# Hash attention with a SiLU MLP on one core: the first head's loads in two parts on two queues, its value sum later, and another order of the query blocks

## Chip, core and metric

One core of one Trainium2 chip. The metric is the device time of one execution in microseconds (us), as a median of several executions. With it each execution has a *span*: the time from the first to the last instruction. Engines: PE (TensorE, matmuls), ACT (ScalarE), DVE (VectorE), POOL (GpSimd), SP (SyncE, which here only issues loads and stores).

## The reference, cut to what matters

```python
# q, k, v: (4, 8, 768, 64) f32; proj: (64, 6); w_in: (512, 2048); w_out: (2048, 512)
q_bits = einsum('bhsd,dk->bhsk', q, proj) > 0          # 6 hash bits of each query
k_bits = einsum('bhsd,dk->bhsk', k, proj) > 0          # and of each key
mask   = bucket(q_bits)[..., :, None] == bucket(k_bits)[..., None, :]
scores = where(mask, q @ k.T / sqrt(64), -1e9)
attn   = softmax(scores)                               # 32 heads of 768 x 768
x      = (attn @ v) as (3072, 512)
h      = x @ w_in
out    = (h * sigmoid(h)) @ w_out                      # (3072, 512) f32
```

## The kernel before

For each head q and k are transposed on PE, multiplied with `proj`, and the signs of the result are appended to q and k as seven further rows ("bit rows"), so that one matmul gives scores that are hugely negative where the hashes differ. A head has 9 *windows* of 512 columns. In each one PE makes scores, ACT the exponential, and three windows later PE the weighted sum with values ("AV"). A matmul of a small constant `dmat` with the sum of all values (the "value sum") gives a query without a matching key the mean of the values. The MLP fills PE between. The whole attention and MLP is one stream on PE, 96% to 100% busy by stage from about 9 us on; the change concerns the first 9 us, in which the first head of 32 is prepared.

```python
    def load_first(h):                       # whole q and k of one head: 192 KB each, SP queue
        for n, src in (("q", q), ("k", k)):
            if h == 0:
                qk_sb[0, n] = ld.tile([P, 2, NJ * D], F32, tag=f"ld{n}", name=f"{n}_row")
            nc.sync.dma_start(out=qk_sb[0, n][:, h],
                              in_=src[0, h].rearrange("(p t) d -> p (t d)", p=P))
    # ... cut ...
    for i in range(2):
        load_first(i)
        load_v(0, slice(i, i + 1))
    load_qk(1)
    load_v(1)
    # ... cut ...
    def warm_up(n):                          # fills PE until data is there
        for _ in range(n):
            nc.tensor.matmul(wps, warm, warm[:, None, :].to_broadcast([P, 4, P]),
                             start=True, stop=True)
    warm_up(5)
    # ... cut: identity, constants, t_first (transposes), cast_first ...
    def proj_first(h):                       # hash projection and signs
        bp = ps.tile([P, 512], F32, tag="m", name="bp_ps", bufs=3)
        for c in range(4):
            e, n = divmod(c, 2)
            x0 = (2 * h + n) * HS
            o = e * (NBIT + 1)
            nc.tensor.matmul(bp[32 * c : 32 * c + 32, 0:HS], pw[:, o : o + 32],
                             qk32[0][:, x0 : x0 + HS], start=True, stop=True)
        bt = btp.tile([P, S], F16, tag="bits", name="bits")
        nc.vector.tensor_scalar(out=bt[:, 0:HS], in0=bp[:, 0:HS],
                                scalar1=sc[:, 0:1], scalar2=sc[:, 1:2],
                                op0=ALU.is_gt, op1=ALU.subtract)
        return bt
    # ... cut ...
    def v_unit(p, heads=(0, 1)):             # values to f16, and their sum, on POOL
        for i in heads:
            # ... cut ...
            nc.gpsimd.tensor_copy(out=vv[:, :, 0:D], in_=src)
            # three adds: vsa, vsb, vs
    # ... cut ...
    def parts(w):                            # which queries a window has
        h, r = divmod(w, NU)
        jp, j = divmod(r, 3)
        if j == 1:                           # queries 512-767 of two key blocks
            return h, [(2 * jp, 512, 256, 0), (2 * jp + 1, 512, 256, 256)]
        return h, [(2 * jp + j // 2, 0, 512, 0)]
    # ... cut: in av(w) ...
            if direct(h):                    # at window 0 of a head
                nc.tensor.matmul(o_ps[h][:, 0:NJ, :], dmat,
                                 vs[:, None, :].to_broadcast([P, NJ, E1]),
                                 start=True, stop=True)
    # ... cut: the order of work for the first head ...
    t_first(0, 0, nc.scalar.copy)
    t_first(0, 1, nc.vector.tensor_copy)
    warm_up(2)
    bt = proj_first(0)
    v_unit(0, (0,))
    # casts on ACT; bit rows on DVE, DVE, ACT, POOL
    t_first(1, 0, nc.scalar.copy)            # head 1, ahead of the first scores on PE
    t_first(1, 1, nc.vector.tensor_copy)
    warm_up(3)
```

The softmax here doesn't subtract the row's maximum and nothing guards it: scores larger than these inputs give would overflow.

## Time and profile before

| | before |
|---|---|
| time, median of 3 runs | 304.34 us (304.14 to 304.92) |
| profiled execution: time, span | 304.54 us, 302.8 us |
| head 0's k landed | 3.90 us |
| first exponential, first AV | 8.42 us, 9.07 us |

Read the profile from the whole to the part: the shares of the engines say which one bounds the kernel, busy times by stage say where that engine is not full, and the chain of work that ended last, in the first 10 us, says what each step there waited for. In a line of the chain the columns are start, length, and engine with tile and source line. The lines themselves stand in the prediction.

### The profile page before, as it was taken

What the parts mean: (1) busy time and instruction counts of PE and PEld (TensorE: products, weight loads), DVE (VectorE), ACT (ScalarE), POOL (GpSimd) and SP (SyncE); (2) the same over time, 40 slices, a digit from 0 to 9 for tenths busy, and PEclk for the clock granted to TensorE, in tenths of its full rate; (3) what the DMA queues carried; (4) which work ended last, traced back from release to release, by engine and by line L of the source; (5) the groups of instructions that cost most, each with busy time, mean ns of one, the idle gap of its engine ahead of it and who ended that gap; (6) DMA issues with size and microseconds to landing.
All of it is one profiled execution on the core that took longest, in us unless ns stands there. A gap on an engine that the chain in (4) does not pass through costs nothing.

```text
span 302.8 us, 7181 instructions
## 1 busy us (share of the span) xinstructions
PE 297.2 (98%) x2710; PEld 175.1 (58%) x2710; DVE 180.3 (60%) x344; ACT 210.2 (69%) x392; POOL 128.3 (42%) x203
## 2 busy tenths in 40 slices
PE   8999999999999999999999999999999999999996
PEld 3675855545665665555565665555566654446653
DVE  5797848899668454854695434854543442764332
ACT  5987989979887686878886766878877732452300
POOL 7589999286617561845149411765111100000000
PEclk9999999999999999999999999999999999999999
DMA  7999997979988737844068226011022003001112
GB/s 195 246 251 196 187 164 123 244 124 163 160 180 137 116 106 194 132 92 134 3 125 131 62 61 202 1 42 31 2 61 63 6 32 95 35 2 69 37 66 73
DMA packets 103170, 32.87 MB, mean 109 GB/s; under 512 B 90656, under 2 KB 100192, under 8 KB 103136
## 3 DMA queue, kind: packets, MB, share of 16 engines
q1 hardware_dynamic: 98752, 28.22, 44.1%
q0 software_dynamic: 4224, 4.19, 9.0%
q8 instruction: 21, 0.34, 0.5%
q14 instruction: 13, 0.11, 0.1%
q10 hardware_dynamic: 160, 0.00, 0.0%
HBM read 27.27 MB, written 6.29 MB: 111 GB/s over the span
## 4 chain that ended last, share of the span: by engine, by line
PE 91%; DVE 6%; ACT 1%; issue 1%; POOL 0%; DVEq 0%; ACTq 0%; POOLq 0%
PE o_ps L496 26%; PE h_ps L461 24%; PE s_ps L366 19%; PE o_ps L398 12%; PE bp_ps L281 3%; DVE g L470 2%; PE tp_ps L185 2%; PE warm_ps L125 1%; PE o_ps L482 1%; ACT u L369 1%; DVE qk L246 1%; PE tp_ps L198 1%; DVE qka L343 1%; PE bp_ps L225 1%; PE o_ps L389 0%
## 5 line engine op out<-in xcount | busy, mean ns | idle before, releaser
L369 ACT ACTIVATE u<-s_ps 128x512 f16<-128x512 f32 x288 | 157.1, 602 | 37.7 <-PE s_ps L366 37.2
L470 DVE SCALAR_TENSOR_TENSOR g<-th,h_ps 128x512 f16<-128x512 f32 x96 | 65.7, 689 | 75.0 <-ACT th L468 75.0
L461 PE MATMUL h_ps<-xT,win 128*128 128x512 f16 (+1 forms) x512 | 97.7, 325 | 0.8 <-DVE g L470 0.8
L398 PEld LDWEIGHTS <-u 128*128 128x128 f16 x1152 | 68.1, 98 | 41.8 <-ACT u L369 8.2
L496 PE MATMUL o_ps<-wout,g 128*128 128x512 f16 x368 | 91.6, 379 | 0.0
L468 ACT ACTIVATE th<-h_ps 128x512 f32<-128x512 f32 x96 | 58.0, 604 | 38.0 <-PE h_ps L461 35.5
L398 PE MATMUL o_ps<-vv,u 128*128 128x65 f16 x1152 | 82.6, 194 | 0.7 <-ACT u L369 0.4
L461 PEld LDWEIGHTS <-win 128*128 128x128 f16 x512 | 49.8, 98 | 32.3 <-issue 1.6
L418 POOL TENSOR_TENSOR x_pr<-osum,rec 128x384 f16<-128x384 f32 x23 | 19.0, 826 | 89.7 <-DVE rec L417 89.2
L496 PEld LDWEIGHTS <-g 128*128 128x128 f16 x368 | 35.8, 98 | 33.6
L366 PE MATMUL s_ps<-qka 71*128 71x512 f16 x192 | 52.6, 327 | 0.1
L366 PE MATMUL s_ps<-qkb 128*128 128x512 f16 x192 | 52.5, 326 | 0.0
L251 POOL TENSOR_SCALAR qka<-qk 64x1536 f16<-64x1536 f32 x15 | 22.0, 1466 | 11.5 <-DVE qk L246 6.5
L501 DVE TENSOR_SCALAR osb<-o_ps 128x512 f32<-128x512 f32 x23 | 15.8, 688 | 15.0 <-PE o_ps L496 15.0
L251 POOL TENSOR_SCALAR qkb<-qk 64x1536 f16<-64x1536 f32 x15 | 22.1, 1471 | 1.2
L262 POOL TENSOR_TENSOR vsa<-v_sb 128x192 f32<-128x192 f32 x32 | 18.9, 592 | 0.0
L260 POOL CAST vv<-v_sb 128x384 f16<-128x384 f32 x32 | 16.2, 507 | 1.8 <-DMA v_sb<-in_v_dram 1.4
L246 DVE STREAM_TRANSPOSE qk<-k_blk 128x768 f32<-128x768 f32 x10 | 15.9, 1589 | 0.3 <-issue 0.3
L246 DVE STREAM_TRANSPOSE qk<-q_blk 128x768 f32<-128x768 f32 x10 | 15.9, 1594 | 0.0
L366 PEld LDWEIGHTS <-qka 71*128 71x128 f16 x192 | 15.5, 97 | 0.7 <-ACT qka L238 0.6
L366 PEld LDWEIGHTS <-qkb 128*128 128x128 f16 x192 | 15.4, 97 | 0.0
L412 DVE TENSOR_TENSOR osum<-o_ps,vsum 128x390 f32<-128x390 f32 x23 | 13.0, 565 | 2.3
(70 smaller groups left out, 162.9 us busy)
## 6 DMA issues: line engine op xcount, KB each, us to landing
out_dram<-osb SPq DMA_DIRECT2D x23, 256.0 KB
v_sb<-in_v_dram SPq DMA_DIRECT2D x15, 384.0 KB
q_blk<-in_q_dram SPq DMA_DIRECT2D x40, 96.0 KB
k_blk<-in_k_dram SPq DMA_DIRECT2D x40, 96.0 KB
win<-in_moe_w_in_dram POOLq DMA_DIRECT2D x4, 512.0 KB, 8.0
wout<-in_moe_w_out_dram POOLq DMA_DIRECT2D x4, 512.0 KB, 6.3
q_sb<-in_q_dram SPq DMA_DIRECT2D x5, 384.0 KB
k_sb<-in_k_dram SPq DMA_DIRECT2D x5, 384.0 KB
```

The costliest lines, as they stand in the source:

```text
L246: nc.vector.transpose(out=dst, in_=qk_sb[p, "qk"[n]])
L251: nc.gpsimd.tensor_scalar(out=dst[rows, :], in0=qk32[p][rows, :], scalar1=CS, scalar2=1.0, op0=ALU.mult, op1=ALU.mult)
L260: nc.gpsimd.tensor_copy(out=vv[:, :, 0:D], in_=src)
L262: nc.gpsimd.tensor_tensor(out=sa, in0=src[:, 0:3], in1=src[:, 3:6], op=ALU.add)
L366: nc.tensor.matmul(sp[:, o0 : o0 + n], t[rows, S + jt * P : S + (jt + 1) * P], t[rows, c0 : c0 + n], start=True, stop=True)
L369: nc.scalar.activation(out=u, in_=sp, func=AF.Exp, scale=ESC)
L398: nc.tensor.matmul(o_ps[h][:, c0 // P + i, :], u[:, o0 + i * P : o0 + (i + 1) * P], vv[:, jt, :], start=(not direct(h) and w % NU == 0 and ...
L418: (nc.vector if direct(h) else nc.gpsimd).tensor_tensor(out=x_pr[p][:, :, par * D : (par + 1) * D], in0=o[:, 0:NJ, 0:D], in1=rec[:, :, Non ...
L461: nc.tensor.matmul(hp[:, j, :], w_in16[:, dt, ft * P : (ft + 1) * P], xT[4 * b + dt][:, c0 : c0 + n], start=(dt == 0), stop=(dt == NDT - 1))
L468: nc.scalar.activation(out=th, in_=hp, func=AF.Tanh, scale=0.5)
L470: after.append(lambda: nc.vector.scalar_tensor_tensor(out=g[ci][:, grp * f : (grp + 1) * f, :], in0=th, scalar=1.0, in1=hp, op0=ALU.add, o ...
L496: nc.tensor.matmul(o2[tt], g[ci][:, ft, ct * P : (ct + 1) * P], w_out16[:, ft, :], start=(ft == 0), stop=(ft == NFT - 1))
```

## The change

Its intent is to start the first head on two thirds of its data. The SP queue brings 256 of the 384 columns of head 0's q and k; the POOL queue brings the rest. Transposes, casts and the projection of the first part can then go ahead. To let the first two windows do without the rest, queries 512 to 767 come third in a group, not second. The value sum of head 0 is moved out of the way of the bit rows on POOL, and its matmul to window 4. The warm-up between the steps, after the first five pieces, is cut from 2560 columns to 640.

```diff
-    def load_first(h):
+    def load_first(h, cols=(slice(0, NJ * D),)):
...
+        for c in cols:
...
+                (nc.gpsimd if h == 0 and c.start else nc.sync).dma_start(
+                    out=qk_sb[0, n][:, h, c], ...)
...
+    load_first(0, (slice(0, 4 * D),))
+    load_v(0, slice(0, 1))
+    load_first(1)
...
     make_identity(nc, ident)
+    load_first(0, (slice(4 * D, NJ * D),))
...
-        if j == 1:
+        if j == 2:
             return h, [(2 * jp, 512, 256, 0), (2 * jp + 1, 512, 256, 256)]
...
-            if direct(h):
+        if direct(h) and w % NU == (0 if h else 4):
...
+    xa, xb = slice(0, 2), slice(2, 3)
+    t_first(0, 0, act, xa)
+    # casts of q's first part on ACT
+    warm_up(1)
+    t_first(0, 1, vec, xa)
+    # casts of k's first part on DVE
+    t_rest()                                  # one transpose each of q's and k's rest
+    # casts of the rest on ACT and POOL
+    v_unit(0, (0,), "v")                      # values to f16, without the sum
+    warm_up(3)
+    bpa, bpb = proj_first(0, xa), proj_first(0, xb)
+    signs_first(0, bpa, xa)
+    # bit rows of the first part on DVE, POOL, ACT
+    signs_first(0, bpb, xb)
+    # bit rows: ACT (first part), DVE, DVE, POOL, POOL (rest)
+    v_unit(0, (0,), "s")                      # the sum
+    t_first(1, 0, act)
+    t_first(1, 1, vec)
+    warm_up(1)
+    nc.vector.memset(QKB[1][0:64, :], 0.0)    # moved here
```

(Cut at the dots; comments stand for loops.)

## The prediction

> **What bounds the kernel now.** I read the page's shares first, then the busy time by stage, then the chain of work that ended last over the first 10 us, then the timelines and waits of single engines there, and last the DMA queues.
>
> The page's busy shares and its chain say that TensorE (PE) is the bound:
>
> ```profile
> PE 297.2 (98%) x2710; PEld 175.1 (58%) x2710; DVE 180.3 (60%) x344; ACT 210.2 (69%) x392; POOL 128.3 (42%) x203
> PE 91%; DVE 6%; ACT 1%; issue 1%; POOL 0%; DVEq 0%; ACTq 0%; POOLq 0%
> ```
>
> By stage, in busy us of each engine, the first 9 us are the part in which PE does little useful work (35 matmuls, of which 10 are warm-up); from 9 us on it is full:
>
> ```profile
> 0.00:9.00 9.00, 7.89 (x35) 3.33 (x35) 5.44 (x47) 5.31 (x10) 6.36 (x16) 1.00 0.76 200
> 9.00:16.00 7.00, 6.93 (x88) 4.51 (x89) 4.62 (x11) 6.28 (x13) 4.05 (x8) 1.00 1.27 246
> 16.00:27.00 11.00, 11.00 (x138) 7.83 (x135) 9.00 (x20) 9.33 (x18) 9.77 (x16) 1.00 1.20 244
> ```
>
> So a change in the first 9 us is worth what it moves the first weighted sum with values (line 398, at 9.07), and, PE being full from there to the end, a shift there should reach the end whole. The chain in the head (start, length, what):
>
> ```profile
> 1.01 2.31 PE warm_ps L125 x5
> 3.32 1.48 PE tp_ps L198 x6
> 4.80 0.79 PE warm_ps L125 x2
> 5.59 0.78 PE bp_ps L225 x8
> 6.37 0.90 PE tp_ps L198 x6
> 7.27 0.65 PE warm_ps L125 x3
> 7.92 0.09 issue
> 8.01 0.39 PE s_ps L366
> ...
> 8.42 0.61 ACT u L369
> ...
> 9.07 0.30 PE o_ps L398 x4
> ```
>
> The names hide that PE's warm-up there is filler: what is really waited for is data, then copies. The transposes of k waited for their load until 3.90, and everything after follows from it: the copy of k on VectorE (DVE) 4.84 to 5.40, hash projection 5.59 to 6.37, signs on DVE 6.44 to 7.12, bit rows to 7.9, first score 8.01, first exponential 8.42. From the waits and the timeline of ScalarE (ACT):
>
> ```profile
> PEld tp_ps L198 <- DMA k_row<-in_k_dram: 0.2, 1, 0.2
> ...
> 7.16 0.51 ACT L238 COPY qka<-bits 7x384 f16<-7x384 f16 x1 [0.25 <-DVE bits L228]
> 7.69 0.48 ACT L201 COPY qk<-tp_ps 128x384 f32<-128x384 f32 x1
> 8.42 2.06 ACT L369 ACTIVATE u<-s_ps 128x512 f16<-128x512 f32 x4 [0.25 <-PE s_ps L366]
> ```
>
> From k's landing (3.90) to the first exponential is 4.52 us. That interval is what the change shortens.
>
> **What the Trainium skill says.** "DMA: Bandwidth & Descriptors", section Latency and other measured facts, gives a first byte after about 0.6 us for a load from the SP queue and about 1 us for one from the POOL queue. The trace is slower on both: the first q load is issued at 0.74 and the queue has no packet before 1.6, and a POOL load of w_in issued at 28.95 (0.96 us of POOL) shows no packet until the slice 31.8 to 32.2; the second, issued at 36.67, shows its first ones between 38.5 and 39. So 1.9 to 2.9 us, for loads with more rows than the new ones. The same page, Issuing engines are not separate DMA queues, says that all queues interleave on the same 16 engines; the trace agrees in so far as both queues have packets in one slice (q0 is POOL's, share of 16 engines last):
>
> ```profile
> q0 software_dynamic: 20, 0.02, 89.6%
> q1 hardware_dynamic: 53, 0.06, 43.4%
> ```
>
> "TensorE: Matmul & The Clock Gate", Part 1, says the array starts at half clock and needs a busy window of about 3.4 us; Part 4 says transposes don't count as busy in the same way. The trace agrees with the first: six transposes take 1.48 us at 3.32 and 0.90 at 6.37, two warm-ups take 0.79 and three later 0.65. The projection, 0.78 at 5.59, takes 0.78 at 9.59 too, so full speed came between 4.8 and 5.6. No run here shows the second.
>
> **The change, part by part.**
> (1) Loads. The SP queue now brings 256 of 384 columns of head 0's q and k, 2 x 128 KB in place of 2 x 192. At the 237 to 258 GB/s of 2 to 4 us the 128 KB less are worth about 0.5 us: k's first part at 3.4. But PE is in warm-ups until 3.32 anyway. The rest, 2 x 64 KB, is issued from POOL after the identity, which ends at 1.46.
> (2) PE's order is: transposes of the first parts, then both transposes of the rest, a 384-column warm-up, and only then the projection of the first part. PE runs matmuls in order, so the projection waits for the POOL loads although it does not read them. This is the hinge. Their landing, an estimate: w_in's issue held POOL 0.8 to 1.0 us, so the second issue starts near 2.3; first packet 1.9 later, the lower end as there are fewer rows, 4.2; 64 KB at half of some 230 GB/s, 0.6. So L = 4.8.
> (3) From L: two transposes at half clock, 2 x 0.25, L+0.5; 384 columns of warm-up 0.2, L+0.7; projection of 256 columns, 0.78 x 2/3 = 0.52, L+1.2; signs: 0.68 less 128 columns at 1.0 ns (copies of 512 and 384 columns take 0.69 and 0.56), 0.55, L+1.85 with 0.1 to start. Then the bit rows: ACT has two in place of one, each about 0.39 (0.51 less 128 columns at 0.94 ns), L+2.65, then its copy of head 1, 0.48, L+3.15, then the exponential at L+3.2. PE meanwhile does the second projection (0.26), six transposes (0.90) and 128 warm-up columns: ready at L+2.45, so the first score is done by about L+2.9, before ACT is free.
> (4) Before, this interval is 4.52; now 3.2: 1.3 us less, from projecting two thirds, from casts done while the rest is still in flight, and from 512 + 3 x 512 columns of warm-up dropped. But it starts at 4.8 and not at 3.90: 0.9 us later. Net 0.4 us earlier: exponential at 8.0 in place of 8.42.
> (5) Value sum of head 0 late: POOL's three adds (0.60 + 0.32 + 0.32) come after the bit rows, and the matmul with the sum moves from window 0 to 4. It takes nothing from PE, as the matmul's 0.17 stays; it frees the way to the first bit row on POOL.
> (6) Queries 512-767 third in a group: lets the first two scores start without the rest. In all 288 windows the columns and weight loads stay: two 256-column scores take 0.22 in the chain, as one of 512 does. Worth 0 in the steady part, give or take 0.2 from where MoE units fall.
> Sum: 304.34 - 0.4 = 303.9.
>
> **Rivals.**
> A: the POOL loads land late and take the place of the wait removed. For it: 2.9 us to the first packet in one case, and the SP queue keeps the DMA engines 83 to 95% busy from 2 us on. Against: a quarter of the rows. At L = 5.6 the exponential starts at 8.8 and the time is 304.7.
> B: POOL becomes the bound of the head. Its two memsets (2.69 us at 1.40) now follow the issues, ending near 5.7; then two casts (0.3 each), the value cast (0.51) and the key bit row (0.37), at 7.3, just where PE is ready (L+2.45 = 7.25). Each 0.1 more on POOL above that is 0.1 later. At worst 304.4.
> C: the clock is released one window later, since 2560 columns of warm-up became 640 and PE may idle before the rest lands. It would add 0.5 to 0.8 us to projection and transposes and double the first scores: 305.2. Against: the five big warm-ups stay. Some 15%.
> D: the head gets faster but the gain is lost later, as ACT is 90% busy from 9 to 16 us. Against: it is also ahead, and PE has no slack to give back a shift to. The opposite, all waits go well (L = 4.3), gives 303.4.
>
> **Range and chances.** Centre 303.9; A and C pull up by about 1, D's opposite down by 0.6, and the three runs before spread over 0.8 us. So 303.0 to 305.0. Two per cent is 6 us, far more than the 9 us head can give or take by these terms: faster 0.01, same 0.98, slower 0.01.
>
> **What would show it.** The DMA wait in the head should be on the POOL loads, at 4.5 to 5.2, ahead of the transposes of the rest; the projection should start at about 5.5 and take 0.5 + 0.3; the first exponential at 7.8 to 8.3 and the first weighted sum at 8.4 to 8.9; from there to the end the same length as before within 0.3 us. Wrong if the first exponential moves by more than 0.8 us either way, if the transposes after 6 us still take 0.25 each (rival C), or if the shift of the head and the shift of the end differ by more than 0.4 us.

## The result and the profile after

The changed kernel took 305.06 us, median of 4 runs (304.91 to 305.89); the kernel before took 304.38 in 4 runs beside it. The ratio is 1.0026, 95% interval 1.0003 to 1.0048: within 2%, but above the predicted 303.0 to 305.0, and slower where 0.4 us faster was expected. (A ratio is the mean time of one kernel's fast runs over the mean of the other's in the same rounds, so not quite the ratio of the medians quoted.) By means, 305.23 is 0.77 us more than 304.46.

The profiled execution took 305.89 us with a span of 303.8, so it is the slowest of the four, and it shows more of the loss than a usual one. First its page, shares and the chain by engine:

```profile
PE 296.3 (98%) x2716; PEld 175.5 (58%) x2716; DVE 181.1 (60%) x348; ACT 210.2 (69%) x394; POOL 130.6 (43%) x209
PE 88%; DVE 6%; ACT 2%; DMA 1%; issue 1%; POOL 0%; DVEq 0%; ACTq 0%; POOLq 0%
```

PE still bounds the kernel and is busy 0.9 us *less* than before, as warm-up was cut. But "DMA 1%" is new in the chain. The first stage of the changed kernel (bounds and length, then busy us and instructions of PE, PEld, DVE, ACT, POOL, then clock, DMA share and GB/s):

```profile
0.00:9.00 9.00, 6.10 (x37) 2.90 (x38) 4.33 (x47) 4.41 (x10) 6.41 (x16) 1.00 0.81 199
```

PE is busy 6.10 us of these 9 where it was 7.89, and not because it finished early. The chain of the changed kernel in its head:

```profile
1.48 0.77 POOL q_row L81
...
2.25 4.02 DMA k_row<-in_k_dram
...
6.31 0.33 PE tp_ps L216
6.64 0.16 PE warm_ps L131
6.81 0.61 PE bp_ps L248 x8
...
7.45 0.56 DVE bits L256
...
8.03 0.40 ACT qka L265
...
8.87 0.48 ACT qk L210
9.35 0.58 ACT u L399
...
9.97 0.29 PE o_ps L429 x4
```

A single transfer, 64 KB of k from the POOL queue, holds the chain from 2.25 to 6.27. All that follows is the sequence that the prediction named: transposes, projection at 6.81 (before 5.59), signs, two bit rows on ACT, ACT's copy of head 1, the exponential. (The chain counts an instruction from the moment at which nothing else held it, so its start can lie up to 0.1 us after the timeline's, which has this exponential at 9.32.) The first AV stands at 9.97 where it was at 9.07. The waits of PE and the DMA issues of the changed kernel (KB, and us from issue to landing) name the same transfer:

```profile
PEld tp_ps L216 <- DMA k_row<-in_k_dram: 1.6, 1, 1.6
```

```profile
q_row<-in_q_dram POOLq DMA_DIRECT2D x1, 64.0 KB, 3.0
k_row<-in_k_dram POOLq DMA_DIRECT2D x1, 64.0 KB, 4.0
```

And k's first part, with a third less in it, landed no earlier. Its transposes waited for it until 4.22 us in this profile, where the whole load had been there at 3.90 (start, us, what was done, and in brackets the idle time before and what ended it; first before, then after the change):

```profile
3.90 0.50 PEld L198 LDWEIGHTS tp_ps<-ident,k_row 128*128 128x128 f32 x3 [0.16 <-DMA k_row<-in_k_dram]
```

```profile
4.22 0.29 PEld L206 LDWEIGHTS tp_ps<-ident,k_row 128*128 128x128 f32 x2 [0.74 <-DMA k_row<-in_k_dram]
```

Both loads were issued at 1.19. In later profiles of the changed kernel this wait ended between 3.8 and 4.0, so 64 KB less of k brought nothing. q's first part did come a little sooner: the first weight load of its transposes starts at 3.00 in place of 3.24. In the first 3 us the SP queue started 210 packets (about one per row of a load) with 0.30 MB before, and 208 with 0.19 MB after. It is tempting to read a pace of rows from this, but the two counts agree only at that moment: by 2.25 us they are 45 and 107.

The shift of the first AV is 0.90 us, that of the span 1.0, and that of the time in this pair 1.35: 0.35 us of the loss lie outside the span, where no line of the profile is. In all runs of the two kernels the time outside the span is 1.78 us for the one before and 2.13 for the changed one (means).

### The profile page after: what moved, and what is told of

Its sections match the earlier page's. It is cut to its first block, busy times and chain, and to the rows that moved or that the text cites. A ratio compares the mean times of both kernels' runs of the same rounds, so it can differ in the third digit from the quotient of the medians.

```text
span 303.8 us, 7208 instructions
## 1 busy us (share of the span) xinstructions
PE 296.3 (98%) x2716; PEld 175.5 (58%) x2716; DVE 181.1 (60%) x348; ACT 210.2 (69%) x394; POOL 130.6 (43%) x209
## 4 chain that ended last, share of the span: by engine, by line
PE 88%; DVE 6%; ACT 2%; DMA 1%; issue 1%; POOL 0%; DVEq 0%; ACTq 0%; POOLq 0%
PE o_ps L528 26%; PE h_ps L493 24%; PE s_ps L396 18%; PE o_ps L429 12%; PE bp_ps L311 3%; DVE g L502 2%; PE tp_ps L193 2%; DMA k_row<-in_k_dram 1%; PE o_ps L514 1%; ACT u L399 1%; DVE qk L273 1%; DVE qka L373 1%; PE o_ps L420 0%; PE bp_ps L248 0%; DVE qkb L370 0%
## 5 line engine op out<-in xcount | busy, mean ns | idle before, releaser
L429 PEld LDWEIGHTS <-u 128*128 128x128 f16 x1152 | 66.8, 98 | 45.6 <-ACT u L399 8.2
L273 DVE STREAM_TRANSPOSE qk<-q_blk 128x768 f32<-128x768 f32 x10 | 15.8, 1579 | 0.0
L273 DVE STREAM_TRANSPOSE qk<-k_blk 128x768 f32<-128x768 f32 x10 | 15.8, 1577 | 0.0
```

Source lines behind the costliest of these rows:

```text
L273: nc.vector.transpose(out=dst, in_=qk_sb[p, "qk"[n]])
L429: nc.tensor.matmul(o_ps[h][:, c0 // P + i, :], u[:, o0 + i * P : o0 + (i + 1) * P], vv[:, jt, :], start=((h == 0 or not direct(h)) and w % ...
```

## Experiments

In what follows "before" is always the kernel before, run on the same chip; its mean is 304.70 to 304.82 us (304.46 in the four runs beside the first result), its mean span 302.93 to 303.05. Its own spans range over 302.4 to 303.7 us. after_again, rest_by_sp, proj_ahead, order_only, quiet_sp, late_and_order, parts_only and warm_small ran on chip 15, whole_loads, warm_fill, pool_early and split_only on chip 0, the others on chip 1. The theories: the rest of head 0 lands late from POOL's queue, and PE's order makes the projection wait behind it (T1 in the expectations); the loss sits in the steady part, from the new order of query blocks (T2); loads here cost by row and issue, so that a split brings nothing earlier (T3); less warm-up makes TensorE's clock rise late (T4); SP's loads, in flight at once, delay the rest (T5), or POOL's queue is slow by itself (T6).

All runs in one table: mean time and span, time outside the span, instructions that the page counts on DVE, and the ratio to before with its 95% interval.

| run | time | span | outside | DVE count | ratio |
|---|---|---|---|---|---|
| after_again | 306.29 | 304.15 | 2.14 | 348 | 1.0048 (1.0029 to 1.0066) |
| rest_by_sp | 305.97 | 303.80 | 2.17 | 348 | 1.0040 (1.0022 to 1.0058) |
| proj_ahead | 305.56 | 303.52 | 2.05 | 351 | 1.0027 (1.0011 to 1.0042) |
| order_only | 304.83 | 303.03 | 1.80 | 344 | 1.0003 (0.9984 to 1.0021) |
| whole_loads | 304.67 | 302.52 | 2.15 | 348 | 0.9993 (0.9979 to 1.0008) |
| warm_fill | 305.15 | 302.98 | 2.17 | 348 | 1.0009 (0.9994 to 1.0024) |
| pool_early | 305.37 | 303.23 | 2.13 | 348 | 1.0016 (0.9999 to 1.0034) |
| split_only | 306.23 | 304.45 | 1.78 | 344 | 1.0037 (1.0018 to 1.0056) |
| late_and_order | 305.13 | 303.35 | 1.78 | 344 | 1.0013 (0.9992 to 1.0033) |
| parts_only | 305.97 | 303.82 | 2.15 | 348 | 1.0045 (1.0014 to 1.0075) |
| warm_small | 304.80 | 303.03 | 1.78 | 344 | 1.0002 (0.9987 to 1.0017) |
| after_third | 304.88 | 302.75 | 2.13 | 348 | 1.0004 (0.9992 to 1.0016) |
| pad_dve | 305.44 | 303.30 | 2.15 | 347 | 1.0022 (1.0003 to 1.0040) |
| pad_pool | 304.55 | 302.80 | 1.75 | 344 | 0.9992 (0.9972 to 1.0012) |
| best | 304.58 | 302.80 | 1.78 | 349 | 0.9993 (0.9980 to 1.0006) |
| best2 | 304.02 | 302.22 | 1.80 | 349 | 0.9978 (0.9966 to 0.9991) |
| after_pad | 304.83 | 303.03 | 1.79 | 349 | 1.0012 (0.9992 to 1.0032) |

All results were correct. One run of after_pad (309.90) was slow and is left out; one of parts_only (307.15, at a clock of 0.994) lifts its mean by 0.4; quiet_sp, a single deliberately slow run, is told below.

### after_again: the changed kernel once more

No edit.

> The changed kernel unaltered, five rounds beside the kernel before, and a second profile. My theory (T1): PE's in-order queue holds the first hash projection behind the transposes of the rest, and the POOL loads of the rest land late and unevenly (6.27 us in the first profile, against 4.8 predicted), so head and total are about 0.6 us longer, with a spread between runs of some 0.5 to 1 us: median 305.0, and the first exponential of the profiled run at landing + 3.0 to 3.2 us. Rival (T2): the loss sits in the steady part, from the new order within a group; then the first exponential could be as early as before and the total still longer.

Measured: 306.37 us median, slower still, all six spans between 303.6 and 304.6. Its chain shows a second thing that can go wrong:

```profile
2.25 3.57 DMA k_row<-in_k_dram
...
6.66 1.44 PE bp_ps L248 x16
8.10 1.47 PE tp_ps L206 x6
```

The rest of k landed at 5.82, earlier than in the first profile. But the 16 projection matmuls took 1.44 us (PE's timeline gives 1.51 for them here, and 0.86 in rest_by_sp below), and six transposes 1.47, as slow as the six at 3.32 in the kernel before (1.48). The clock rose only after 9.5 (the packed trace keeps the clock's changes, which `prof` does not print: full speed from 10.01 on), and the first exponential stood at 10.14. That is rival C of the prediction, seen in one profile. The column of the granted clock does not show it (it reads 1.00 from 5 to 9.5 us in this trace too); the durations of equal instructions do. What follows: the loss has more than one source, and its size varies from execution to execution.

### rest_by_sp: the rest by the SP queue, right after the first parts

```diff
-                (nc.gpsimd if h == 0 and c.start else nc.sync).dma_start(
+                nc.sync.dma_start(
-    load_first(0, (slice(0, 4 * D),))
+    load_first(0, (slice(0, 4 * D), slice(4 * D, NJ * D)))
```

> The only edit: the rest of head 0's q and k (2 x 64 KB) is issued from the SP queue directly after the first parts, ahead of v. T1 (the POOL queue is what is late): the rest lands at about 4.3 to 4.8, the first exponential at 7.4 to 7.9, total 303.3 to 303.9. Rival T3 (early loads run at a pace per row and not per byte, so that four loads of 128 short rows land as late as four of long ones): the rest lands near 5.2, first exponential 8.3, total about 304.3, no gain over before. T2 (steady part): the head is early but the total stays near 305.

Measured: 306.02 us, by means 0.31 below the changed kernel and 1.15 above before. PE's wait for the rest ended at 5.15, and now head 1's k, whose issue had moved two places back in the queue, landed at 7.79 (start, us, engine and line, then in brackets the idle time before and what ended it):

```profile
7.92 0.52 PE L205 MATMUL tp_ps<-ident,k_row 128*128 128x128 f32 x3 [0.84 <-DMA k_row<-in_k_dram]
```

PE takes matmuls in order, and head 1's transposes stand ahead of the first scores; so these wait for a load that they don't read. The first exponential stood at 8.76. The expected 303.3 to 303.9 was missed: T1 alone doesn't hold. Without POOL's queue the rest is 0.7 us earlier than in after_again (same chip) and 1.1 earlier than in the first profile, but two more issues on SP's make a later load late.

### split_only: the kernel before, its first loads split in two by SP

```diff
-            nc.sync.dma_start(out=qk_sb[0, n][:, h], in_=... whole)
+        for c in (slice(0, 4 * D), slice(4 * D, NJ * D)) if h == 0 else ():
+            for n, src in (("q", q), ("k", k)):
+                nc.sync.dma_start(out=qk_sb[0, n][:, h, c], in_=...[:, c])
```

> The kernel before with one edit: head 0's q and k loaded in two parts each, all four by the SP queue; the work is as before and needs both parts. T3 (early loads run at a pace per row, issue by issue): the last part lands at about 5.1 in place of 3.9 to 4.0, head 1's k at 7.8 in place of 6.7; first exponential 9.2 to 9.6, total 305.3 to 305.7. If bytes set the pace: lands at 4.0 to 4.3, total under 304.8. Also looked at: the time outside the span (total less span), which is 1.8 us for before and 2.1 for the change: it stays at 1.8 if it has to do with the work in parts, and goes to 2.1 if with the number of loads.

Measured: 306.07 us, span 1.4 us above before. The work is that of the kernel before, and so are the bytes:

```profile
2.31 2.97 DMA k_row<-in_k_dram
...
6.65 1.44 PE bp_ps L230 x8
8.09 1.47 PE tp_ps L203 x6
```

k's last part lands at 5.28 in place of 3.90. PE idles for it, the clock rises late again (projection 1.44 where it took 0.78), and the first exponential stands at 10.92. That is later than the 9.2 to 9.6 expected, and the total exceeds 305.7, because of the clock. The landing is what T3 said, and the issue times say which half of T3 it is: whole, k was issued at 1.19 and landed 2.7 us later; its last part was issued at 2.31, as the fourth load, and landed 3.0 us later. So of the 1.4 us 1.1 come from the later issue, and a load of 64 KB takes no less time than one of 192. That is a pace of issues; a pace of rows is not shown apart from it. That k's first part is no earlier was seen in the changed kernel.

### quiet_sp: the rest from POOL while the SP queue is held

SP's other loads were made to wait for three tiny POOL memsets (into the tiles they fill), placed after POOL's two large ones, so that they start only after 5.5 us. Slow on purpose (310.97 us, one run): only the landing counts.

```diff
+    for t in (v_sb[0], qk_sb[0, "q"][:, 1:2], qk_sb[0, "k"][:, 1:2]):
+        nc.gpsimd.memset(t[:, :, 0:1], 0.0)
+    load_v(0, slice(0, 1)); load_first(1); ...    # moved here
```

> The changed kernel, with the SP queue's later loads (v, head 1, pair 1) held back behind three tiny memsets at the end of POOL's, so that POOL's two loads of the rest have the DMA engines nearly to themselves until about 5.5 us. One look, for the landing alone; the total will be several us worse on purpose. If traffic of the SP queue makes the landing late (T5): k's rest lands by 4.4 to 4.8 (2.2 to 2.5 us after its issue). If it is the software path itself (T6): at 5.5 to 6.3 as in the changed kernel, 3.3 us or more after the issue.

The DMA issue of this run:

```profile
k_row<-in_k_dram POOLq DMA_DIRECT2D x1, 64.0 KB, 2.5
```

Alone, the transfer takes 2.5 us from issue to landing, the length that the prediction had assumed (2.3 to 4.8). Beside SP's loads it took 4.0, 3.6, 2.8 and 2.8 us in four profiles of the changed kernel and of after_pad, whose loads are the same, and 3.6 in proj_ahead and 2.7 in warm_fill, which also share them. On chip 15, that of this run, the two profiles with SP's loads have 3.6, so T5 fits there with 1.1 us, from one profile; on chips 0 and 1 SP's loads add only 0.2 to 0.3, and T5's own forecast for after_third was missed (below). So SP's traffic is a part of the delay, and not shown to be all of it. In the first profile, of the 64 packets of POOL's queue three lie between 5 and 6 us, all others earlier, so that it was the last few that came late:

```profile
q0 software_dynamic: 3, 0.00, 1.7%
```

By the packed trace two of these three carry 4 bytes; in after_again the last four, at 5.1 to 5.5, all do.

### proj_ahead: the projection of the first part ahead of the rest

In the changed kernel, PE gets the projection of part one (and DVE, POOL, ACT its signs and bit rows) ahead of the transposes of the rest; the rest's copy and q casts go to DVE.

```diff
+    bpa = proj_first(0, xa)
+    signs_first(0, bpa, xa)
+    for n, e, copy in ((0, 0, vec), (1, 0, pool), (0, 1, act), (1, 1, act)):
+        bits_first(0, n, e, copy, xa)
     t_rest()
-    bpa, bpb = proj_first(0, xa), proj_first(0, xb)
+    t_first(1, 0, act)
+    bpb = proj_first(0, xb)
```

> POOL loads kept; the projection, signs and bit rows of the first part stand ahead of the transposes of the rest in the program, the copy and q casts of the rest go to DVE so that ACT's bit rows don't wait behind them. T1: the projection of the first part starts at 5.4 although the rest lands near 6; the first exponential at about 7.9 to 8.2 and hardly moves with the landing; total 303.7 to 304.1 and a smaller spread. If instead the landing is not what holds the head (T2, or POOL as the bound, rival B of the prediction), the first exponential stays near 9 and the total near 305.

Measured: 305.45 us; the expected 303.7 to 304.1 was missed. The projection ran at 4.92 to 5.56, as wanted, but DVE's two casts of k stood ahead of the signs and ended only at 6.17; the first exponential came at 8.72, not at 7.9 to 8.2, and the third score waited on DVE's bit rows until 8.96. The hinge that the prediction named was real, and opening it moved the wait to DVE.

### pool_early: POOL's issues ahead of its identity

```diff
+    load_first(0, (slice(4 * D, NJ * D),))     # right after the warm-up's memset
     warm_up(20)
     make_identity(nc, ident)
-    load_first(0, (slice(4 * D, NJ * D),))
```

> The changed kernel with the two POOL issues moved ahead of the identity, 0.5 us earlier. If the landing is a fixed time after the issue[...]: it comes 0.5 us earlier, at 5.3 to 5.8, and the total is 0.4 us below the change's. If it is set by the SP queue's traffic on the same DMA engines: it stays at 5.8 to 6.3, total unchanged.

Measured: 305.14 us. The issues came only 0.19 us earlier (1.30 in place of 1.49), not 0.5. PE's wait for k's rest ended at 4.92, below both forecasts; but without the edit the rest landed at 4.94 in warm_fill, so this run doesn't decide between them. The profiled execution had its first exponential at 8.20, a span of 302.6. What then held the chain was DVE:

```profile
5.08 1.28 DVE L235 TENSOR_SCALAR qka<-qk 64x256 f16<-64x256 f32 x2
```

Two casts take 1.28 us here, beside POOL's memset that runs to 5.83. In the first profile of the changed kernel they took 0.59, almost clear of that memset (5.40 to 5.99, memset to 5.51), and in after_third, half beside it, 0.94. "SBUF — State Buffer", section Who interferes with whom, says that DVE in its faster modes and POOL lock each other out of a shared port pair; the three durations agree with that, though no run shows in which mode these casts ran.

### warm_fill: more warm-up ahead of the rest

```diff
+    warm_up(12)
     t_rest()
```

> The changed kernel with 12 x 128 columns of warm-up put ahead of the transposes of the rest, where PE waits for POOL's loads anyway. Clock theory (T4: part of the loss, on this chip, is that the clock is released at about 10 us in more executions since warm-up was cut from 5120 to 3200 columns and PE idles): the slow executions (spans of 304.5) vanish, spans are 303.0 to 303.9, median total 305.3 to 305.7. If the clock has no part: as the change itself, 306.2, both levels still there.

Measured: 305.15 us, five spans of 302.7 to 303.5, mean as before. With PE kept busy, the clock was up before the projections of its profile (first 8 in 0.61 us). But the warm-up itself took until 5.90, after the rest had landed, and the first exponential stood at 9.02.

### warm_small: the kernel before with the changed kernel's small warm-ups

```diff
-    warm_up(5)
+    warm_up(20)     # pieces of up to four blocks of 128 columns, in all three places
-    warm_up(2)
+    warm_up(4)
-    warm_up(3)
+    warm_up(1)
```

(The memset of `QKB[1]` is moved too, as in the change.)

> The kernel before with only the change's small moves: warm-up of 4 x 128 and 128 columns in place of 2 x 512 and 3 x 512, and the second memset of a key tile moved from 3 us to after head 1's transposes. T4 (less warm-up lets the clock be released a window later in some executions): two levels of span, the upper near 304, mean span 0.2 to 0.6 above before's. If warm-up has no part: spans as before, 302.4 to 303.7. Outside the span 1.8.

Measured: 304.80 us, ratio 1.0002. Less warm-up by itself costs nothing, so T4 falls in its simple form.

The clock's changes in the packed traces say more. In the profiles whose head has before's loads and matmuls, full speed begins at 4.10 us (order_only), 5.40 (before), 6.00 (pad_pool), 6.79 (pad_dve) and 6.81 (late_and_order), and their spans follow it: 302.4, 302.8, 303.1, 303.4 and 303.5 us; so do the first exponentials, 8.20 to 9.10. So most of the spread of before, and half a microsecond either way in any single profile of a head, goes with the moment of the clock. Of the other profiles, quiet_sp apart, only after_again (10.01) and split_only (10.36) are later than 7.00. The records' stretches are whole multiples of 3.41 us. One such step before their rise, at 6.60 and 6.95, these two could have had it as late_and_order did; but PE, idle for a split load, had been busy for only 2.31 and 2.74 of the 3.41 us before, where it was busy for 2.85 or more before the first rise of every other profile that records one. So the late rise goes with two things together, where the steps of 3.41 us fall and how idle PE was. No experiment tests it, and one record doesn't fit so simply: quiet_sp stays at half speed until 17.68, although PE was busy all through the step from 10.85 to 14.27.

### order_only: the kernel before with queries 512 to 767 third

```diff
-        if j == 1:
+        if j == 2:
```

> The kernel before with one edit: queries 512-767 third in a group in all heads, nothing else. T1: worth nothing: 304.3 to 304.5, ratio to before within 0.0007 of 1, first exponential at 8.4 as before. T2 (the loss is in the steady part): 304.9 to 305.1, as the whole change.

Measured: ratio 1.0003, span as before; the first exponential of its profile stood at 8.20, with an early clock (above). No gain or loss of the order of the query blocks by itself is seen, as predicted, within the interval's 0.2%.

### late_and_order: that order and the late value sum, in the kernel before

```diff
+        if direct(h) and w % NU == (0 if h else 4):      # matmul with the sum, at window 4
-    v_unit(0, (0,))
+    v_unit(0, (0,), "v")
     # bit rows
+    v_unit(0, (0,), "s")
```

> The kernel before with the new order within a group and the late value sum of head 0, without loads or work in parts. By the prediction both are worth 0 on PE: mean span within 0.4 us of before. Also for the 0.35 us outside the span: 1.8 us outside if these have no part in it, 2.1 if they are its cause.

Measured: 305.29 us, ratio 1.0013 with an interval that holds 1. Its profiled execution had a late clock for this head (8 projections 1.38 us), so this says only that no gain of the late sum is seen in the kernel before.

### whole_loads: the changed kernel with whole first loads

```diff
-    load_first(0, (slice(0, 4 * D),))
+    load_first(0)
-    load_first(0, (slice(4 * D, NJ * D),))
```

> The changed kernel with one edit: head 0's q and k are loaded whole, each by one load of the SP queue, as before; the work in parts, the order and the late value sum stay. T1 (what costs is the landing of the split rest, and the interval of about 3.05 us from its landing to the first exponential is sound): the rest is there with the first parts at about 4.0, its transposes end by 4.9, the first exponential comes at 7.4 to 7.8, against 8.4 (8.2) before, and the span is 301.8 to 302.3 at an early clock release: total 303.8 to 304.2, at most that of before. Rival (working in parts is itself slower: more and smaller instructions on ACT, POOL and DVE): the first exponential stays at 8.5 or later, total over 305.

Measured: 304.83 us; the span fell to 302.52, 0.52 us below before (303.04), so everything in the change except the split is good for about half a microsecond of span, and the split is what costs. (The changed kernel did not run in this call. Beside before in its own calls its mean span was 1.10 longer in after_again and 0.27 shorter in after_third, which puts the split at 0.2 to 1.6 us.) The time gained only 0.15 by means, as 2.15 us lie outside the span. I had expected the exponential at 7.4 to 7.8. In the profiled execution (span 302.8) it was at 8.42, since a warm-up of 384 columns stood in PE's order between the landed data and a projection at half speed (the clock rose at 7.00):

```profile
5.22 0.32 PE warm_ps L131
5.54 1.06 PE bp_ps L247 x8
```

### parts_only: whole loads, work in parts, value sum early

```diff
-        if direct(h) and w % NU == (0 if h else 4):
+            if direct(h):                                # at window 0, as before
-    v_unit(0, (0,), "v")
+    v_unit(0, (0,))
-    v_unit(0, (0,), "s")
```

> The run with whole loads, but with the value sum back to early (before POOL's bit rows, and its matmul first in window 0). If the late sum matters as the prediction says (it frees POOL's bit row): POOL reaches its first bit row about 1.2 us later, the first exponential comes at 8.6 to 9.3 in place of 8.4, span about 0.4 to 0.8 longer than with whole loads and a late sum (302.5). Outside the span: 2.1 if the work in parts is the cause of the 0.35 us, 1.8 if the late sum is.

Measured: 305.62 us, span 1.3 us above whole_loads by means (0.9 without the run of 307.15), though not on the same chip. The chain shows POOL in the way:

```profile
7.91 0.32 POOL vs L294
...
8.29 0.40 POOL qka L264
...
8.74 0.40 PE s_ps L395
```

The bit row on POOL comes after the sum, and the score after the bit row. So the late sum is needed where the work goes in parts; where it doesn't, no gain was seen.

### after_third, pad_dve and pad_pool: the time outside the span

after_third is the changed kernel once more. The two others are the kernel before with tiny memsets that nothing reads:

```diff
+    pad = cst.tile([P, 4], F32, name="pad")
+    for i in range(3):                         # pad_pool: range(2), nc.gpsimd
+        nc.vector.memset(pad[:, i : i + 1], 0.0)
```

> The changed kernel again, a third profile, beside the best version on one chip. Traffic theory (T5): k's rest lands 3.5 to 4.1 us after its issue at 2.25, that is at 5.8 to 6.3; first exponential 9.0 to 9.4, or 10.1 where the clock comes late; mean span 303.1 to 304.2, 2.13 us outside it.

> The kernel before with three more tiny DVE memsets early, where DVE has slack. For the time outside the span alone: the work in parts has three DVE instructions more. If the number of DVE instructions makes the 0.35 us: 2.1 us outside; if not: 1.8. Span as before.

> The kernel before with two more tiny POOL memsets after the identity. For the time outside the span alone: the work in parts has two POOL instructions more. If their number makes the 0.35 us: 2.1 us outside; if not: 1.8. Span as before.

Measured: after_third 304.85 us beside 304.84 for before, though its span, 302.75, is 0.27 us *below* before's 303.02. In its chain the rest landed at 5.08, and the exponential stood at 8.16, close to the 8.0 predicted. Every forecast of T5 for this run (landing at 5.8 to 6.3, exponential from 9.0 on, span over 303.1) was missed on the early side:

```profile
2.25 2.83 DMA k_row<-in_k_dram
...
8.16 0.58 ACT u L399
```

pad_dve put the time outside the span from 1.78 to 2.15 us; pad_pool left it at 1.75. (By its page the changed kernel has four DVE and six POOL instructions more, not three and two, so pad_pool doesn't try its whole number.) Three memsets of one column at the start of the kernel are not work after its last instruction. So the changed kernel pays 0.35 us for its number of DVE instructions, or for how they are laid out, and not for what they do. The span of pad_dve (two runs) is within before's range.

### after_pad: the changed kernel with one more DVE instruction

```diff
+    pad = cst.tile([P, 4], F32, name="pad")
+    nc.vector.memset(pad[:, 0:1], 0.0)
```

> The changed kernel with one more instruction: a memset of 128 x 1 elements on VectorE that nothing reads, ahead of the loads. Its page will count 349 instructions on VectorE, as in best, instead of 348. If the 0.35 us that the changed kernel takes outside the span hang on how many instructions VectorE has (344 and 349 gave 1.78 us; 347 and 348 gave 2.15; 351 gave 2.05), the time outside the span falls from 2.13 to 1.78 us and the total from about 305.0 to about 304.6 us, with the span unchanged at 302.7 to 304.0 us. If they hang on something else in the changed kernel (the two issues from GpSimd's queue, more semaphores), the time outside stays at 2.13 us.

Measured: in its three fast runs the time outside the span is 1.79 us, as expected if the count matters. One instruction *more* takes 0.34 us *away*. By the count on DVE in all runs: 344 and 349 give 1.75 to 1.80 us, 347 and 348 give 2.13 to 2.17, 351 gives 2.05. The three fast runs gave 304.83 us on average, with a span of 303.03: no better in total than after_third, as the span happened to be 0.28 us longer.

### best and best2: keeping what helped

best is whole_loads without the warm-up ahead of the projection, and with one bit row on DVE instead of ACT. best2 also moves the value-sum matmul of *both* first heads to window 8 and, on POOL, puts head 1's casts ahead of the two sums.

```diff
     # best, against whole_loads
-    warm_up(3)
     bpa, bpb = proj_first(0, xa), proj_first(0, xb)
+    bits_first(0, 1, 1, vec, xa)               # was on ACT
     # best2, against best
-        if direct(h) and w % NU == (0 if h else 4):
+        if direct(h) and w % NU == (0 if h > 1 else 8):
-    v_unit(0, (0,), "s")
...
-        v_unit(0, (1,))
+        v_unit(0, (1,), "v")
+        v_unit(0, (0,), "s")
+        v_unit(0, (1,), "s")
```

> The run with whole loads, with two edits from its timeline: the 384-column warm-up ahead of the first projection goes, and the second key bit row goes from ACT to DVE (0.40 to about 0.22 us), so that ACT's copy of head 1 and the first exponential come 0.4 to 0.5 earlier. If the chain in the head sets the time: first exponential at 7.6 to 8.1 (8.42 with whole loads), mean span 301.9 to 302.3 (302.52), total 304.0 to 304.4, below before's mean of 304.8 by 0.1 to 0.3%. If another wait takes their place (POOL's bit row, bits of the second part): span as with whole loads.

> The kernel best (whole first loads; no warm-up between the transposes and the projection; the second key bit row on VectorE) with the value-sum matmul of both first heads moved to window 8, and on GpSimd head 1's key casts and value-bits work ahead of the two value sums. Best had its first exp at 7.86 us where the kernel before had 8.42, and had lost that lead by 15.8 us; the wait in its trace was PE's for GpSimd's value sum at 14.02 to 14.36 us, and a score that waited for VectorE's bits. If that wait is what gave the lead back, moving the matmul later keeps some of it: mean span 302.3 to 302.6 us where best had 302.80, time outside the span 1.78 us as in best, total 304.1 to 304.4 us, 0.4 to 0.7 below the kernel before. If the lead goes in another place (the order of ScalarE's and VectorE's work for the second pair of heads), the span stays at 302.7 to 302.9 us and the total at 304.5 to 304.7 us.

Measured: best 304.50 us with a span of 302.80, both short of what was expected, and an interval that holds 1. best2 304.01, better than expected, with all five runs between 303.91 and 304.16, below all nine of before (304.28 to 305.27). Best had its first exponential at 7.86, 0.56 ahead of before, and had lost it by 15.8. PE's timeline of best shows where, and below it that of best2:

```profile
14.36 0.33 PE L419 MATMUL o_ps<-vs,dmat 128*128 128x390 f16 x1 [0.17 <-POOL vs L294]
...
15.74 0.30 PE L428 MATMUL o_ps<-vv,u 128*128 128x65 f16 x4
```

```profile
13.46 0.33 PE L419 MATMUL o_ps<-vs,dmat 128*128 128x390 f16 x1
...
15.19 0.30 PE L428 MATMUL o_ps<-vv,u 128*128 128x65 f16 x4
```

In best, PE waited for POOL's sum of head 1. (Another 0.17 us of the lead went to head 0's sum matmul: in before it ran at 8.65, while PE waited for the first exponential; in best it stands in the full stream, at 11.29.) In best2 that sum is not waited for, and the AV that follows the hash projection of the second pair of heads starts at 15.19 and not at 15.74 (15.74 in the kernel before, too). The lead of 0.55 us reaches the end: mean span 302.22 against 302.93. Best2 beats before by 0.22% (interval 0.09% to 0.34%), and its slowest run lies below every run of the changed kernel, after_pad's among them.

## Why the prediction was wrong

**The bound, and that a shift of the head carries to the end: right.** First AV 0.90 us later, span 1.0 later. PE has no slack to give or take in the steady part, except where a new wait appears in the stage right after (best).

**Step (1), the first part: wrong.** It put 128 KB less at 0.5 us, from a rate in bytes. k's first part was there at about 4.2 (3.8 to 4.0 in later profiles) and not at 3.4, and the whole load had been there at 3.90.

**Step (2), the landing of the rest: this term failed.** That the projection waits there was right: it started 0.54 us after the landing. The size was not: 2.5 us from the second issue, made up of a first packet after 1.9 and 0.6 for the bytes, gave L = 4.8. Measured: 6.27, 5.82 and 5.08 in three profiles. The 2.5 is what the transfer takes when the SP queue is held (quiet_sp); beside SP's loads it takes 2.7 to 4.0. The first packets of POOL's queue lay between 3.0 and 3.25 us, 1.5 to 1.8 after the first issue began, so the 1.9 was not too short; the time lies in the rest of the transfer. Nearly all the bytes had gone before 4.8, as step (2) had it. What it lacked is the end of a load: its last, almost empty packets, which came as late as 5.85, and 0.3 to 0.5 us more from the last packet to the landing. That the 2.5 agree with quiet_sp is in part luck: there the last packet started before 4.5, earlier than step (2) had it, and the landing came 0.4 us after it.

**Step (3), from L to the exponential: right.** 3.2 predicted; 9.35 less 6.27 is 3.08, and 3.08 in after_third too. Its pieces were right to 0.2 us: transposes and warm-up shorter (0.54 in place of 0.7), the first projection 0.61 in place of 0.52, each bit row on ACT 0.42 with its gap in place of 0.39.

**Step (4), the net: wrong by the landing.** The interval shrank by 1.44 us where 1.3 were predicted, but began 2.37 later and not 0.9. This gives 0.93 later in place of 0.4 earlier, more than the 0.8 that the prediction named as its sign of being wrong. Where L was 5.08 (after_third), the exponential came at 8.16, 0.26 earlier than before.

**Step (5), the late sum: right** that it frees POOL's bit row (parts_only), not that it takes nothing from PE. Before, the sum's matmul ran at 8.65, while PE waited for the first exponential, and is not in the chain; in the changed kernel it stands in the chain at 12.84, with its 0.17 us. **Step (6), the order: right,** worth 0 within the noise (order_only).

**Rivals.** A happened in the profiled run, even beyond the size given it (L = 5.6). C happened in after_again, but not by less warm-up (warm_small): PE was idle for a split load, and the clock's steps of 3.41 us fell late, as in late_and_order, where a busy PE kept the rise at 6.81. That is what the records suggest; no experiment shows it. D was not seen in the changed kernel, but in best.

**What the prediction did not have at all: 0.35 us outside the span.** It is about half of the loss of 0.77 us by means. pad_dve puts it on the kernel before, after_pad takes it from the changed kernel. That it goes with the number of DVE instructions is seen for five numbers, and set on purpose for two of the steps; why it does, and with what period, is open. It was not to be had from the profile, all lines of which lie inside the span, and the prediction took the time as the span plus a constant.

What stays open besides: whether the landing depends on the chip or on the execution. With the same loads it was 5.82 and 5.87 on chip 15 (after_again, proj_ahead), 4.94 on chip 0 (warm_fill), 5.08 and 5.09 on chip 1 (after_third, after_pad). That points to the chip or the call, and the mean span of the changed kernel points the same way, 304.15 on chip 15 and 302.75 on chip 1, with before alike on both (303.05 and 303.02); with one call each, it is not shown. The loss by means was 0.1 to 1.5 us.

## What to carry to other kernels

In the head of this kernel, splitting a load hardly made its first part arrive sooner: k's loads landed 2.6 to 3.0 us after their issue, whether of 192, 128 or 64 KB. Before you count on a split, look at when each part will be issued and how long loads take from issue to landing, and not at their bytes; and take the time of a small transfer from a moment when the other queues are as busy as they will be. What helped was to split the *work* and not the load, to drop the warm-up between data and projection, to take waits for off-path engines (a value sum) out of PE's order, and to follow the lead in the trace until it is lost. For differences under half a microsecond, look at the time outside the span first: an unrelated instruction more or less can give or take 0.35 us there.

## What the Trainium skill lacked or had wrong

- "DMA: Bandwidth & Descriptors", Latency and other measured facts: its first byte after about 1 us for a POOL load is early for this case. The issue began at 1.48 us and the first packet lay between 3.0 and 3.25, so 1.5 to 1.8 us.
- "SBUF — State Buffer", The DMA setup-cost knee: about 2 us plus bytes over 436 GB/s gives, as an estimate, 2.15 us for 64 KB. Alone it took 2.5 us, and 2.7 to 4.0 beside SP's loads; the fit has no term for other traffic.
- "TensorE: Matmul & The Clock Gate", Part 1: the steps of 3.41 us in the clock's records agree with its free-running window, but its scatter of 0.5 us is too small here: full speed came at 4.10 to 6.81 us in heads with the matmuls of before, and after 10 in after_again and split_only.
- No page that I found relates the time outside the span to the number of instructions of an engine: 1.78 us with 344 or 349 on VectorE, 2.15 with 347 or 348, 2.05 with 351.
